# A new list of moves behind the front, four more key tiles for VectorE, and reads of two score banks at once

## The chip, the cores and the metric

The kernel runs on one core of one Trainium2 chip. The metric is the device time of one execution in microseconds; the median of three runs is 638.3 us (638.2 to 638.46).

## The reference

x is 2048 x 512. It is normalised row by row, goes through multi-query attention with 32 heads of 16 and one shared key and value head, and through a dense block of width 1792. The result is x + attention * silu(dense).

```python
xn = _layernorm(x, axis=-1)
q = (xn @ wq).reshape(B, S, H, Dh)                   # H = 32, Dh = 16
k, v = xn @ wk, xn @ wv
scores = jnp.einsum("bhqd,bkd->bhqk", q, k) * (Dh ** -0.5)
p = _softmax(scores, axis=-1)
s = jnp.einsum("bhqk,bkd->bhqd", p, v).transpose(0, 2, 1, 3).reshape(B, S, H * Dh) @ wo
h = _silu(jnp.einsum("bsd,df->bsf", xn, w1))
g = _silu(jnp.einsum("bsf,fd->bsd", h, w2))
return x + s * g
```

There are 2048 x 2048 x 32 scores, and each needs an exponential. That is most of the work.

## The kernel before

**Tiling.** The queries are cut into 4 chunks of 512 and the heads into 8 groups of 4, which makes 32 groups (chunk, heads). In each group the 2048 keys are cut into 16 key tiles of 128. A block is the scores of one key tile for one head: 128 keys by 512 queries, one PSUM bank of float32. One key tile of a group has 4 blocks, one for each head. The heads of 16 channels lie in strips of 32 rows, so TensorE is split into 4 row tiles for the scores (contraction over 32 rows, four heads side by side) and into 4 column tiles for everything that is summed over 128 rows.

**Two ways to the exponential.** The first is ScalarE. `fill_A` (L665) lets TensorE fill two blocks into psA, of which there are two copies of 1024 columns, and `exp_A` (L668, the activation is L674) takes the exponential of all 1024 columns into pa_sb. Two such steps make a key tile. The second is VectorE. `fill_block` (L1311) fills one block into one of four banks: D and D1 (the two halves of psD), F (psF) or O (psO). `exp_D` (L709, the instruction is L714) adds a constant to the scores, cuts at zero and writes 16-bit integers, which, read as bf16, are a rough exponential. When all four blocks of the tile are done, `shift` (L731, L739) makes POOL add a constant to the integers twice, which gives two copies that are shifted in phase; the three together, with weights in vaug_sb, approximate the exponential. So a key tile on ScalarE costs 2 exponentials and 4 matmuls against the values, and one on VectorE costs 4 reads on VectorE, 2 additions on POOL and 12 matmuls against the values.

**Quads.** `emit_quad` (L753, the matmul is L769) issues four such matmuls, one for each column tile, which run side by side into psO. `next_quad` (L1374) picks, for each of the four heads, the finished block with the earliest time `at` that the Python clock gave it. A dense quad (`emit_job`, L1049, through `columns`, L404) is likewise four matmuls side by side: the projection of q, the two layers of the dense block and the output projection. A change of TensorE between row tiles and column tiles happens at every alternation of a burst of score matmuls and a group of quads. The dense results go through tanh on ScalarE (L1116) and are multiplied on VectorE.

**Order.** Every engine works through its own queue in order. All queues are written out when the program is made, by `Sched.op`, which sets the semaphores from the data that an instruction reads and writes, and books a time for it on a clock in Python (`Sched.model`, L96). The clock itself leaves no instruction on the chip. Up to 30 us of booked ScalarE time a greedy planner picks the moves (the front); then `follow` (L1448) plays the moves written down in the string ORDER, and `finish` (L1378) those in TAIL. The letters that matter here:

- R0 or R1: fill psA for heads 0 and 1, or 2 and 3, of the next key tile; e: the exponential of it on ScalarE
- o: open a key tile for VectorE (taken from the end of the group's list), the second digit is one of four buffers; f: fill one block of it, the first digit is the bank (0 D, 1 D1, 2 F, 3 O), the second the tile and the head
- x: VectorE reads the oldest filled block; y: it reads the two oldest in one instruction of 1024 columns, which `exp_D` has a form for
- v: one quad against the values; J and d: open a dense job, and issue so many of its quads; t: its tanh; E: VectorE's step behind it
- 1 to 4: the four steps that normalise a group; H: one of the eight split bursts of the last group's first four key tiles, which `run_part` (L681, the matmul is L692) makes with parts of the queries; P, q, n and the rest: the last output rows

R and f that follow each other on TensorE's queue make one burst of row tiles, v and d one group of quads. A burst that comes to the same row tile twice needs a second pass.

Of the kernel before, what the change touches and what calls it, by code (L numbers as in the profile page):

```python
# [35 lines left out]
class Sched:  # L36
# [3 lines left out]
    SWITCH, FLY, SEM = 0.104, 0.172, 0.048  # L40

    def __init__(self):
        self.queues = {}
        self.done = {}
        self.clock = {}
        self.snap = {}
        self.last_w = {}
        self.readers = {}
        self.flagged = {}
        self.lanes = {}  # L50
        self.at = {}
        self.free = dict(pe=1.2, a=1.7, v=0.85, gp=0.7, sp=0.7)
        self.act_end = 0.0
        self.act_ends = []
        self.pe_mode, self.pe_last, self.pe_len, self.pe_tiles = None, 1.0, 0.0, set()
        self.pe_runs = []
        self.gp_runs, self.tt_runs = [], []

# [23 lines left out]
    def ready(self, eng, reads=(), writes=()):  # L82
        return max([self.at[d] for d in self.deps(eng, reads, writes).items()], default=0.0)
# [12 lines left out]
    def model(self, eng, lane, cost, r):  # L96
        if lane:
            t = max(self.free[eng], r) + 0.05
            self.free[eng] = t + (0.86 if eng == "gp" else 0.5)
            return t + (cost or 2.25)  # L100
        if eng == "pe":
            mode, tiles, cols = cost or ("full", [None] * 4, 128)
            t = r
            for tile in tiles:
                if mode != self.pe_mode:
                    t = max(t, self.pe_last + self.pe_len + self.SWITCH)
                    self.pe_tiles = set()
                elif tile is not None and tile not in self.pe_tiles:
                    t = max(t, self.pe_last + 0.004)
                else:  # L110
                    t = max(t, self.pe_last + self.pe_len + 0.003)
                    self.pe_tiles = set()
                self.pe_tiles.add(tile)
                self.pe_mode, self.pe_last, self.pe_len = mode, t, max(cols, 60) / 2400.0
                self.pe_runs.append((t, t + self.pe_len))
            self.free[eng] = t
            return t + cols / 2400.0 + self.FLY + self.SEM
        if eng == "a":
            n = cost or 512
            t = max(r, self.free["a"], self.act_end - 0.428)  # L120
            self.free["a"] = t
            self.act_end = max(t + 0.274 + n / 1200.0, self.act_end + 0.0635 + n / 1200.0)
            return self.act_end + self.SEM
        t = max(r, self.free[eng] - (0.084 if eng == "v" else 0.0))
        if eng == "v" and isinstance(cost, tuple):

            t = max(r, self.free[eng] - 0.13)
            end = t + cost[0]
            for a, b in self.gp_runs[-6:]:
                if a < t - 0.1:  # L130
                    end = max(end, b + cost[0] - 0.13)
            self.tt_runs.append((t, end))
            self.free[eng] = end
            return end + self.SEM
        end = t + (cost or 0.4)
        if eng == "gp" and cost and cost > 1.0:
            for a, b in self.tt_runs[-3:]:
                if a <= t + 0.1 and b > t:
                    end = max(end, b + 0.89)
            self.gp_runs.append((t, end))  # L140
        self.free[eng] = end
        return end + self.SEM

    def op(self, eng, fn, reads=(), writes=(), lane=None, cost=None):
        who = lane or eng
        if lane:
            self.lanes[lane] = eng
        n = self.done.get(who, 0)
        self.done[who] = n + 1
        deps = self.deps(eng, reads, writes)  # L150
        self.at[(who, n)] = self.model(eng, lane, cost, max([self.at[d] for d in deps.items()], default=0.0))
        clk = self.clock.setdefault(eng, {})
        waits = []
        cand = [(f, m) for f, m in deps.items() if clk.get(f, -1) < m]
        for f, m in cand:
            implied = False
            for f2, m2 in cand:
                if (f2, m2) != (f, m) and self.snap[(f2, m2)].get(f, -1) >= m:
                    implied = True
            if not implied:  # L160
                waits.append((f, m))
        for f, m in cand:
            for g, k in self.snap[(f, m)].items():
                if clk.get(g, -1) < k:
                    clk[g] = k
            if clk.get(f, -1) < m:
                clk[f] = m
        for f, m in waits:
            self.flagged.setdefault(f, set()).add(m)
        self.snap[(who, n)] = dict(clk)  # L170
        self.queues.setdefault(eng, []).append((fn, waits, who, n))
        for r in reads:
            self.readers.setdefault(r, {})[who] = n
        for w in writes:
            self.last_w[w] = (who, n)
            self.readers[w] = {}
        return who, n
# [36 lines left out]
def bass_recurrent_scan__grouped_kv_mqa__dense_activation_silu__prompt_kernel(  # L214
# [60 lines left out]
        K=(0.2, 3.0, 0.65, 10, 1.2, 2.0, 0, 24, 0.2, 3, 3, 0.0, 9, 0.43, 0, 0.33, 0, 0),  # L275
# [15 lines left out]
        a=(0.3, 3.0, 0.65, 10, 1.2, 2.0, -4, 24, 0.2, 3, 3, 0.04, 9, 0.43, 0, 0.33, 0, 0),  # L291
# [7 lines left out]
    TAIL = "vvHvvHPvvvvHHq0q0q0q0q1q1q1q1n0PPn1n0n1PPPq2q2q2n0n1n0q2PPr0r1n2C1n1n2n2G0Pr2Pn2PG2Pr3C3X1M1Y1A2A0M3Z1A3"  # L299
    ALPHA = "".join(chr(x) for x in range(35, 127) if x != 92) + "".join(chr(x) for x in range(192, 255))  # L300

    with ExitStack() as es:
        def sb(name, shape, dt=BF16):
# [44 lines left out]
        K = Sched()  # L348
        op = K.op


        op("gp", lambda e: e.memset(ident[:], 0.0), writes=["ident"])
        op("gp", lambda e: e.affine_select(out=ident[:], in_=ident[:], compare_op=ALU.not_equal, fill=1.0,
                                           base=0, pattern=[[-1, P]], channel_multiplier=1),
           reads=["ident"], writes=["ident"])
# [19 lines left out]
        for j in range(NPH + 1):  # L375
# [12 lines left out]
           reads=["wkn", "wkp"], writes=["wkp"])  # L388
# [7 lines left out]
        def load_w2():  # L396
            op("sp", lambda e: e.dma_start(of, xf), writes=["outx"], lane="lox", cost=20.0)
            op("sp", lambda e: e.dma_start(w2_sb[:], B_w2.rearrange("(ft p) n -> p ft n", p=P)), writes=["w2"], lane="lw2", cost=9.0)
# [229 lines left out]
        def bank_ap(b, m=NQ):  # L628
            if b == "O":
                return psO[:, :]  # L630
            return psF[:, :] if b == "F" else psD[:, NQ * (b == "D1"):NQ * (b == "D1") + m]
# [26 lines left out]
        def held(key):  # L658
            return waiting.get(key, 0) > 0
# [160 lines left out]
        def task(kind, run, cost, reads, writes, need=(), **kw):  # L820
            need = [n for n in need if not (n[0] in ("gn3", "gn4", "wmm", "add") and n[1] < 0)]
            tasks.append(dict(kind=kind, run=run, cost=cost, reads=reads, writes=writes, need=need, **kw))
# [289 lines left out]
        def emit_tanh():  # L1112
            jb, b = jst["tanh"].pop(0)
            n = state["nt"]
            state["nt"] += 1
            d = op("a", lambda e: e.activation(t_sb[:, n % 2, :], bank_ap(b), ACT.Tanh, scale=0.5 if jb[0] == "h" else 0.25),  # L1116
                   reads=[b], writes=[("t", n % 2)], cost=NQ)
            K.at[d] -= 0.06
            task(jb[0], evac, 0.679, jb=jb, bank=b, n=n, reads=[b, ("t", n % 2)], writes=[])
# [231 lines left out]
        def settled():  # L1351

            return not front and not shifts and all(("ag", t) in tok for t in tiles(NC - 1)) and ("kT", 1, NC - 1) in tok and K.act_end >= HANDOVER and \
                not any(tk["kind"] in ("st", "ag", "nm", "T", "K", "V") for tk in tasks)
# [154 lines left out]
        while not followed:  # L1509
# [3 lines left out]
            if not followed and settled():  # L1513
                if not w2_asked:
                    load_w2()
                    w2_asked = True
                follow(ORDER)
                followed = True
                continue
            t = max(now, min(K.pe_next("col"), K.pe_next("full")))  # L1520
# [7 lines left out]
            if tanh_ready(K.act_end - TGATE if more else t):  # L1528
                emit_tanh()
# [5 lines left out]
            if more:  # L1535
# [4 lines left out]
                if TWIN and K.pe_mode == "row" and not front and release() <= K.pe_next("row") + 0.12:  # L1540
                    slots, t = 0, K.pe_next("row")
# [5 lines left out]
            if slots > 0:  # L1547
                gi = state["g"]
                full = blocked or sum(held(("pa", k)) for k in range(NPA)) >= HOLD
# [7 lines left out]
                end = gi < NGRP and t >= gdone[gi] - PVWAIT and owed[gi] <= ENDQ  # L1557
# [23 lines left out]
            else:  # L1581
                now = 0.0
        finish(TAIL)
        last = {}
# [36 lines left out]
```

## Time and profile before

| | |
|---|---|
| median of 3 runs | 638.3 us |
| span of the profiled execution, first to last instruction | 635.8 us |
| TensorE matmuls busy | 628.8 us, 8227 |
| ScalarE busy | 625.9 us, 722 instructions |
| VectorE busy | 605.5 us, 1049 instructions |
| POOL busy | 435.6 us, 438 instructions |
| listed part, from its first burst to its last split burst | 29.5 to 622.7 us |

The page gives the span of the profiled execution and no other time of it. A row of the grouped view has line, engine, operation, output and inputs by name, shapes and count; then the busy time in us and the mean of one in ns; then the time for which the engine stood idle before them and what ended it. A row of the timeline has start and length in us, then the same names, and "x2" where rows that follow each other are drawn together. A sum over windows has for each engine the busy time in that stretch and the count.

### The profile page before, as it was taken

The numbers are of one execution on the slowest core, as the hardware profiler recorded it, in microseconds if no ns is written. First come the engines' busy times: TensorE is split into PE (matmuls) and PEld (weight loads), VectorE is DVE, ScalarE is ACT, GpSimd is POOL, SyncE is SP. The second block draws the span as 40 slices with busy tenths as digits, with TensorE's granted clock in tenths as the row PEclk, the third lists the DMA queues.
The fourth block names the chain that finished last, engine by engine and source line by source line (L and its number), as shares of the span: only waits on it lengthen the run. The fifth ranks groups of instructions, "written<-read, shape, count | busy, mean of one in ns | idle before, by whom it ended". The sixth has DMA issues, their size and how long they took to land.

```text
span 635.8 us, 18804 instructions
## 1 busy us (share of the span) xinstructions
PE 628.8 (99%) x8227; PEld 195.9 (31%) x8227; DVE 605.5 (95%) x1049; ACT 625.9 (98%) x722; POOL 435.6 (69%) x438
## 2 busy tenths in 40 slices
PE   8999999999999999999999999999999999999997
PEld 3433333332323222223223332223223233223323
DVE  8999999999999999999999999999999999999993
ACT  8999999999999999999999999999999999999996
POOL 6466665767667778777666876678767776776771
PEclk9999999999999999999999999999999999999999
DMA  6380000000000100000000000001000000000012
GB/s 185 117 283 2 2 2 2 2 3 1 2 2 2 19 1 11 10 2 2 1 3 2 1 3 2 2 10 18 10 3 2 2 2 1 3 1 2 3 18 53
DMA packets 10083, 12.51 MB, mean 20 GB/s; under 512 B 2288, under 2 KB 9456, under 8 KB 9968
## 3 DMA queue, kind: packets, MB, share of 16 engines
q1 hardware_dynamic: 7840, 9.34, 4.5%
q0 software_dynamic: 1728, 1.57, 2.1%
q8 instruction: 64, 1.05, 0.7%
q10 hardware_dynamic: 432, 0.39, 0.2%
q14 instruction: 19, 0.16, 0.1%
HBM read 8.95 MB, written 4.19 MB: 21 GB/s over the span
## 4 chain that ended last, share of the span: by engine, by line
PE 84%; ACT 9%; DVE 5%; DMA 0%; issue 0%
PE psO L769 32%; PE psA L643 27%; PE psF L404 20%; ACT pa_sb L674 8%; DVE ph_sb L714 3%; PE psD L643 2%; DVE x_sb L714 1%; ACT t_sb L1116 0%; PE psA L692 0%; DMA x_sb<-in_A_x_dram 0%; PE psD L507 0%; PE psD L476 0%; PE psF L643 0%; PE psD L533 0%; DVE stats_sb L424 0%
## 5 line engine op out<-in xcount | busy, mean ns | idle before, releaser
L674 ACT ACTIVATE pa_sb<-psA 128x1024 bf16<-128x1024 f32 x630 | 592.6, 1072 | 1.9 <-PE psA L643 0.6
L739 POOL INT64_ADD ph_sb<-ph_sb x304 | 316.5, 1056 | 131.2 <-DVE ph_sb L714 131.0
L714 DVE TENSOR_SCALAR ph_sb<-psD 128x512 int16<-128x512 f32 x521 | 336.5, 681 | 10.4 <-PE psD L643 8.5
L769 PE MATMUL psO<-ph_sb,vaug_sb 128*32 128x512 bf16 x1824 | 227.5, 383 | 0.1
L769 PE MATMUL psO<-pa_sb,vaug_sb 128*32 128x512 bf16 (+1 forms) x1292 | 201.5, 378 | 0.0
L643 PE MATMUL psA<-qT_sb,kTa_sb 32*128 32x512 bf16 x632 | 122.1, 384 | 0.1
L739 POOL INT64_ADD x_sb<-x_sb x90 | 93.3, 1055 | 41.6 <-DVE x_sb L714 41.4
L643 PE MATMUL psA<-qT_sb,kTb_sb 32*128 32x512 bf16 x612 | 118.4, 384 | 0.3 <-ACT pa_sb L674 0.3
L643 PE MATMUL psD<-qT_sb,kTb_sb 32*128 32x512 bf16 x335 | 113.5, 384 | 0.0
L643 PE MATMUL psD<-qT_sb,kTa_sb 32*128 32x512 bf16 x339 | 110.9, 385 | 0.0
L714 DVE TENSOR_SCALAR x_sb<-psD 128x512 int16<-128x512 f32 x153 | 100.8, 682 | 6.1 <-PE psD L643 5.3
L769 PE MATMUL psO<-x_sb,vaug_sb 128*32 128x512 bf16 x540 | 96.4, 383 | 0.0
L769 PEld LDWEIGHTS psO<-ph_sb,vaug_sb 128*32 128x32 bf16 x1824 | 55.8, 95 | 57.5 <-issue 35.1
L643 PEld LDWEIGHTS psA<-qT_sb,kTa_sb 32*128 32x128 bf16 x632 | 29.7, 91 | 122.0 <-ACT pa_sb L674 92.2
L404 PE MATMUL psF<-w_sb,u_sb 128*32 128x512 bf16 x896 | 66.2, 384 | 0.0
L643 PEld LDWEIGHTS psA<-qT_sb,kTb_sb 32*128 32x128 bf16 x612 | 28.7, 91 | 121.0 <-ACT pa_sb L674 98.1
L404 PE MATMUL psF<-xnT_sb,w_sb 128*32 128x512 bf16 x896 | 64.7, 383 | 0.0
L769 PEld LDWEIGHTS psO<-pa_sb,vaug_sb 128*32 128x32 bf16 x1292 | 50.2, 95 | 33.5 <-issue 24.2
L714 DVE TENSOR_SCALAR ph_sb<-psF 128x512 int16<-128x512 f32 x70 | 47.7, 681 | 0.0
L1116 ACT ACTIVATE t_sb<-psF 128x512 bf16<-128x512 f32 x72 | 45.9, 638 | 0.0
L1135 DVE SCALAR_TENSOR_TENSOR u_sb<-t_sb,psF 128x512 bf16<-128x512 bf16 x56 | 38.0, 678 | 0.2
L643 PEld LDWEIGHTS psD<-qT_sb,kTa_sb 32*128 32x128 bf16 x339 | 28.8, 91 | 2.3 <-DVE ph_sb L714 0.4
(121 smaller groups left out, 397.1 us busy)
## 6 DMA issues: line engine op xcount, KB each, us to landing
w_sb<-in_B_w_dram SPq DMA_DIRECT2D x2, 1792.0 KB, 10.9
x_sb<-in_A_x_dram SPq DMA_DIRECT2D x3, 512.0 KB, 5.2
out_dram<-ob_sb POOLq DMA_DIRECT2D x12, 128.0 KB, 3.0
wop_sb<-in_A_wo_dram SPq DMA_DIRECT2D x1, 512.0 KB, 4.1
wq_sb<-in_A_wq_dram SPq DMA_DIRECT2D x1, 384.0 KB, 6.1
out_dram<-ob_sb SPq DMA_DIRECT2D x3, 128.0 KB, 2.4
x_sb<-in_A_x_dram SPq DMA_DIRECT2D x2, 128.0 KB, 2.6
x_sb<-in_A_x_dram ACTq DMA_DIRECT2D x2, 128.0 KB, 2.8
```

What stands on the lines that cost most here:

```text
L404: r = e.matmul(bank[32 * i:32 * i + 32, :], lhsT=w, rhs=rhs, start=start, stop=stop, tile_position=(0, 32 * i), skip_group_check=True)
L643: return e.matmul(ap, lhsT=kT_sb[g % 2][32 * i:32 * i + 32, kt * P:(kt + 1) * P], rhs=qT_sb[32 * i:32 * i + 32, c % 2, g // 2, :], start=T ...
L674: d = op("a", lambda e: e.activation(pa_sb[:, sl, :], psA[k][:, :], ACT.Exp, scale=ESCALE), reads=["A%d" % k], writes=[("pa", sl)], cost=2 ...
L714: d = op("v", lambda e: e.tensor_scalar(ph_ap(0, sl, 512 * pos, 512 * pos + m), src, float(PH_ONE + PH_BIAS), 0.0, op0=ALU.add, op1=ALU.ma ...
L739: d = op("gp", lambda e, j=j: e.int64_add(ph_ap(j, sl, 0, 4 * NQ).bitcast(I64), ph_ap(0, sl, 0, 4 * NQ).bitcast(I64), PH_SHIFT[j] * 0x0001 ...
L769: r = e.matmul(psO[32 * i:32 * i + 32, cs], lhsT=vaug_sb[:, p["v"], p["kt"], DH * (gi % 2):DH * (gi % 2) + 32], rhs=p["ap"], start=s0, sto ...
L1116: d = op("a", lambda e: e.activation(t_sb[:, n % 2, :], bank_ap(b), ACT.Tanh, scale=0.5 if jb[0] == "h" else 0.25), reads=[b], writes=[("t ...
L1135: op("v", lambda e: e.scalar_tensor_tensor(out=dst, in0=t_sb[:, n % 2, :], scalar=1.0, in1=src, op0=ALU.add, op1=ALU.mult), reads=tk["read ...
```

## The change

The class of the clock gets a second mode, `fine`, which is switched on just before `follow`. In it a dependency between TensorE and VectorE, and between VectorE and POOL, has a lag of its own; TensorE, ScalarE, VectorE and POOL are booked with other constants; and the result of a tanh is put earlier by 0.022 instead of 0.06. ORDER is replaced as a whole, and TAIL has three more quads between the sixth and the seventh split burst. The functions that play the moves are unchanged.

Counted from the two strings:

| moves in ORDER | before | after |
|---|---|---|
| e, exponentials of 1024 columns (H included) | 605 | 597 |
| R, fills of psA | 601 | 593 |
| o, key tiles for VectorE | 195 | 199 |
| f, fills for VectorE: D, D1, F, O | 783: 335, 335, 90, 23 | 799: 329, 329, 108, 33 |
| x, reads of one block | 784 | 704 |
| y, reads of two blocks | 0 | 48 |
| v, quads against the values | 887 | 892 |
| dense quads | 556 | 556 |
| t, tanh | 72 | 72 |
| groups of quads between bursts | 595 | 569 |
| of 1, 2, 3, 4, 5, 6 quads | 76, 263, 183, 73, 0, 0 | 122, 164, 182, 58, 38, 5 |
| bursts with two fills of psA | 10 | 28 |
| second passes in bursts | 11 | 31 |
| quads in TAIL against the values, before its last split bursts | 8 | 11 |

Of the 48 places with y, the next burst fills F alone among VectorE's banks in 43, O alone in 3, D and D1 in one and none in one.

```diff
@@ -38,6 +38,7 @@
 
 
     SWITCH, FLY, SEM = 0.104, 0.172, 0.048
+    LAG = {("pe", "v"): 0.0325, ("v", "gp"): 0.0405}
 
     def __init__(self):
         self.queues = {}
@@ -55,6 +56,10 @@
         self.pe_mode, self.pe_last, self.pe_len, self.pe_tiles = None, 1.0, 0.0, set()
         self.pe_runs = []
         self.gp_runs, self.tt_runs = [], []
+        self.fine, self.pe_pos = False, 0
+
+    def when(self, d, eng):
+        return self.at[d] + (self.LAG.get((d[0], eng), 0.0) if self.fine else 0.0)
 
     def deps(self, eng, reads, writes):
         deps = {}
@@ -80,7 +85,7 @@
         return deps
 
     def ready(self, eng, reads=(), writes=()):
-        return max([self.at[d] for d in self.deps(eng, reads, writes).items()], default=0.0)
+        return max([self.when(d, eng) for d in self.deps(eng, reads, writes).items()], default=0.0)
 
     def activity(self, t, window=3.4):
 
@@ -98,6 +103,24 @@
             t = max(self.free[eng], r) + 0.05
             self.free[eng] = t + (0.86 if eng == "gp" else 0.5)
             return t + (cost or 2.25)
+        if eng == "pe" and self.fine:
+            mode, tiles, cols = cost or ("full", [None] * 4, 128)
+            t = r
+            for tile in tiles:
+                end = self.pe_last + self.pe_len
+                if mode != self.pe_mode:
+                    t = max(t, end + (0.098 if mode == "row" else 0.1012))
+                    self.pe_tiles, self.pe_pos = set(), 0
+                elif tile is not None and tile not in self.pe_tiles:
+                    t = max(t, self.pe_last + 0.0033)
+                else:
+                    self.pe_pos += 1
+                    t = max(t, end + (0.003 if mode != "col" or self.pe_pos == 1 else -0.0075))
+                    self.pe_tiles = set()
+                self.pe_tiles.add(tile)
+                self.pe_mode, self.pe_last, self.pe_len = mode, t, max(cols, 60) / 2400.0
+            self.free[eng] = t
+            return t + cols / 2400.0 + 0.2125
         if eng == "pe":
             mode, tiles, cols = cost or ("full", [None] * 4, 128)
             t = r
@@ -115,6 +138,12 @@
                 self.pe_runs.append((t, t + self.pe_len))
             self.free[eng] = t
             return t + cols / 2400.0 + self.FLY + self.SEM
+        if eng == "a" and self.fine:
+            n = cost or 512
+            t = max(r, self.free["a"], self.act_end - 0.428)
+            self.free["a"] = t
+            self.act_end = max(t + 0.1707 + n / 1200.0, self.act_end + 0.0632 + n / 1200.0)
+            return self.act_end + 0.055
         if eng == "a":
             n = cost or 512
             t = max(r, self.free["a"], self.act_end - 0.428)
@@ -131,15 +160,15 @@
                     end = max(end, b + cost[0] - 0.13)
             self.tt_runs.append((t, end))
             self.free[eng] = end
-            return end + self.SEM
+            return end + (0.0565 if self.fine else self.SEM)
         end = t + (cost or 0.4)
         if eng == "gp" and cost and cost > 1.0:
             for a, b in self.tt_runs[-3:]:
                 if a <= t + 0.1 and b > t:
                     end = max(end, b + 0.89)
             self.gp_runs.append((t, end))
-        self.free[eng] = end
-        return end + self.SEM
+        self.free[eng] = end - (0.02 if self.fine and eng == "gp" else 0.0)
+        return end + (0.0565 if self.fine else self.SEM)
 
     def op(self, eng, fn, reads=(), writes=(), lane=None, cost=None):
         who = lane or eng
@@ -148,7 +177,7 @@
         n = self.done.get(who, 0)
         self.done[who] = n + 1
         deps = self.deps(eng, reads, writes)
-        self.at[(who, n)] = self.model(eng, lane, cost, max([self.at[d] for d in deps.items()], default=0.0))
+        self.at[(who, n)] = self.model(eng, lane, cost, max([self.when(d, eng) for d in deps.items()], default=0.0))
         clk = self.clock.setdefault(eng, {})
         waits = []
         cand = [(f, m) for f, m in deps.items() if clk.get(f, -1) < m]
@@ -295,8 +324,8 @@
     NF, F_FROM, F_LEFT, F_LATE, DENSE_END, HOLD, F_BEHIND = 14, 0.05, 9, 3, 0.97, 10, 0
 
     HANDOVER = 30.0
-    ORDER = "xvR0eJ#2d1R1f11f00ed3xxR0o02f16evE#vR1f01exJ$2d2xR0f13ed2xvE$R1f00f11eR0xeJ%2d4xR0o13f02f13eE%vxR1eJ&2d4xR1f00f11tev
...
-R1f01f20evxR0f13evxvvxR1f01eJÄ2d2xR0o00f12ed2xR1f00eEÄvvxR0f13eJÅ2d1xvR1f01ed3xR0o01f12eEÅvR1f00exJÆ2d31R0f13exvvxR1f01ed1xvR0o02f12e2vEÆvR1f00exJÇ2d2xR0f13ed13vxR1f01ed1xvvHeEÇvvHevvHevvHe"
-    TAIL = "vvHvvHPvvvvHHq0q0q0q0q1q1q1q1n0PPn1n0n1PPPq2q2q2n0n1n0q2PPr0r1n2C1n1n2n2G0Pr2Pn2PG2Pr3C3X1M1Y1A2A0M3Z1A3"
+    ORDER = "R0xf11f01exJ$2d2R1xf10exd2R0E$o02f03evvR1xf10evR0xf22o03f07evxvf11xR1eJ#2d2xR0f02exd2vR1E#f10f01evxvR0xo02f12evR1xf2
...
+f03evxvvR0xf12o03f23xevvvR1xf00evR0xf12evxvR11f01eJÃ2d3R1x2o00f10f31ed1d1R0xxf02ed3R0xf13ed1R1xo01f01f30exd2f12xR0exd3vvR13o02f04f15teR1xevvvxvvEÃvR0f03f12evHexJÇ2xd3vd1HeEÇvf03HeJÆ2xd4HeEÆ"
+    TAIL = "vvHvvHPvvvvvvvHHq0q0q0q0q1q1q1q1n0PPn1n0n1PPPq2q2q2n0n1n0q2PPr0r1n2C1n1n2n2G0Pr2Pn2PG2Pr3C3X1M1Y1A2A0M3Z1A3"
     ALPHA = "".join(chr(x) for x in range(35, 127) if x != 92) + "".join(chr(x) for x in range(192, 255))
 
     with ExitStack() as es:
@@ -1115,7 +1144,7 @@
             state["nt"] += 1
             d = op("a", lambda e: e.activation(t_sb[:, n % 2, :], bank_ap(b), ACT.Tanh, scale=0.5 if jb[0] == "h" else 0.25),
                    reads=[b], writes=[("t", n % 2)], cost=NQ)
-            K.at[d] -= 0.06
+            K.at[d] -= 0.022 if K.fine else 0.06
             task(jb[0], evac, 0.679, jb=jb, bank=b, n=n, reads=[b, ("t", n % 2)], writes=[])
 
         def add_x(tt, src, key):
@@ -1514,6 +1543,7 @@
                 if not w2_asked:
                     load_w2()
                     w2_asked = True
+                K.fine = True
                 follow(ORDER)
                 followed = True
                 continue
```

2 lines of the change are left out of this document (1 added, 1 removed).

## The prediction

> **What bounds the kernel now.** I read the page first: the shares of the engines, the chain that ended last and the costliest groups.
>
> ```profile
> span 635.8 us, 18804 instructions
> PE 628.8 (99%) x8227; PEld 195.9 (31%) x8227; DVE 605.5 (95%) x1049; ACT 625.9 (98%) x722; POOL 435.6 (69%) x438
> ...
> PE 84%; ACT 9%; DVE 5%; DMA 0%; issue 0%
> ...
> L674 ACT ACTIVATE pa_sb<-psA 128x1024 bf16<-128x1024 f32 x630 | 592.6, 1072 | 1.9 <-PE psA L643 0.6
> L739 POOL INT64_ADD ph_sb<-ph_sb x304 | 316.5, 1056 | 131.2 <-DVE ph_sb L714 131.0
> L714 DVE TENSOR_SCALAR ph_sb<-psD 128x512 int16<-128x512 f32 x521 | 336.5, 681 | 10.4 <-PE psD L643 8.5
> ...
> L714 DVE TENSOR_SCALAR x_sb<-psD 128x512 int16<-128x512 f32 x153 | 100.8, 682 | 6.1 <-PE psD L643 5.3
> ```
>
> Three engines are over 95%. Then the sums over windows: all of the listed part (29.4 to 620), and the stretch where VectorE is fullest.
>
> ```profile
> core 0: us, PE busy (x) PEld busy (x) DVE busy (x) ACT busy (x) POOL busy (x), PEclk, DMA share, GB/s
> 29.40:620.00 590.60, 590.14 (x7733) 177.79 (x7729) 573.52 (x960) 589.42 (x674) 415.93 (x404) 1.00 0.05 12
> ...
> 200.00:300.00 100.00, 99.54 (x1295) 29.51 (x1291) 99.16 (x168) 100.00 (x114) 75.67 (x74) 1.00 0.05 7
> ```
>
> In the listed part ScalarE stands still for 1.2 us of 590.6 and VectorE for 17.1 us; TensorE's clock is full. ScalarE's instructions overlap, so its floor has to come from the pitch, which a timeline shows:
>
> ```profile
> 299.48 0.60 ACT L1116 ACTIVATE t_sb<-psF 128x512 bf16<-128x512 f32 x1
> ...
> 299.95 3.79 ACT L674 ACTIVATE pa_sb<-psA 128x1024 bf16<-128x1024 f32 x4
> ...
> 613.29 12.98 ACT L674 ACTIVATE pa_sb<-psA 128x1024 bf16<-128x1024 f32 x14
> ```
>
> Fourteen exponentials in 12.98 us, the last 1.07 long: a pitch of (12.98 - 1.07)/13 = 0.916 us. A tanh holds the engine for 299.95 - 299.48 = 0.47, say 0.48 us. The old list has 605 exponentials and 72 tanh: 605 x 0.916 + 72 x 0.48 = 588.8 us.
>
> TensorE needs its own count, since its busy share hides waits. The timeline of TensorE alone shows its rhythm, a burst of score matmuls (psA, psD) and then quads:
>
> ```profile
> 602.69 0.39 PE L643 MATMUL psA<-qT_sb,kTa_sb 32*128 32x512 bf16 x2
> ...
> 603.56 0.39 PE L643 MATMUL psA<-qT_sb,kTa_sb 32*128 32x512 bf16 x2
> ...
> 605.30 0.39 PE L643 MATMUL psA<-qT_sb,kTa_sb 32*128 32x512 bf16 x2
> ...
> 606.45 0.39 PE L643 MATMUL psA<-qT_sb,kTa_sb 32*128 32x512 bf16 x2
> 606.56 0.38 PE L643 MATMUL psD<-qT_sb,kTb_sb 32*128 32x512 bf16 x1
> ...
> 607.21 0.39 PE L643 MATMUL psA<-qT_sb,kTb_sb 32*128 32x512 bf16 x2
> ...
> 608.30 0.39 PE L643 MATMUL psA<-qT_sb,kTb_sb 32*128 32x512 bf16 x2
> ```
>
> A burst with two quads takes 0.87 (602.69 to 603.56, and 605.30 - 602.69 is three of them), with three quads 1.09 (607.21 to 608.30). So a further quad is 0.22, and a burst with one quad 0.65; a second pass in a burst, one more set of 512 columns, I put at 0.21. At 606.56 the psD fill begins 0.11 after its burst where others follow at once: it waits inside the burst for VectorE to give the bank back, and this counts as busy. The old list has 595 groups of quads with 1443 quads and 11 second passes: 595 x 0.648 + 848 x 0.22 + 11 x 0.21 = 574.5 us. Its first and last burst:
>
> ```profile
> 29.49 0.39 PE L643 MATMUL psA<-qT_sb,kTa_sb 32*128 32x512 bf16 x2
> ...
> 620.09 0.39 PE L692 MATMUL psA<-qT_sb,kTb_sb 32*128 32x256 bf16 x4
> ...
> 622.69 0.39 PE L692 MATMUL psA<-qT_sb,kTb_sb 32*128 32x256 bf16 x4
> ...
> 626.02 0.70 PE L692 MATMUL psA<-qT_sb,kTb_sb 32*128 32x128 bf16 x16
> ```
>
> 622.69 - 29.49 = 593.2 us. ScalarE's floor is 4.4 us below that, TensorE's 18.7 us. So ScalarE sets the pace, and what TensorE has left over goes into waits inside its bursts.
>
> **The change, part by part.** *Four more key tiles to VectorE.* ScalarE loses 8 exponentials: 8 x 0.916 = 7.3 us, all of it on the path that sets the pace. VectorE gets 16 blocks, POOL 8 additions (8.4 us at 1056 ns on an engine that is 69% busy and so hides them; without cover each would make its quad late by a microsecond), TensorE 8 quads net of the list and the tail (1.8 us).
>
> *The new grouping on TensorE.* 569 groups, 1448 quads, 31 second passes: 569 x 0.648 + 879 x 0.22 + 31 x 0.21 = 368.7 + 193.4 + 6.5 = 568.6 us, 5.9 less than before. 26 fewer alternations give it; the second passes take back 4.2. Against ScalarE's new floor, 597 x 0.916 + 72 x 0.48 = 581.4, TensorE then has 12.8 us for waits instead of 14.3: ScalarE stays the pace setter as long as waits do not grow.
>
> *Blocks read two at a time.* No instruction of the trace reads two blocks, so its price is bounded:
>
> ```profile
> 251.02 1.89 DVE L714 TENSOR_SCALAR ph_sb<-psD 128x512 int16<-128x512 f32 x3
> ...
> L484 DVE COPY xnT_sb<-psD 128x1024 bf16<-128x1024 bf16 x4 | 2.7, 682 | 0.0
> ...
> L519 DVE CAST kTa_sb<-psD 128x256 bf16<-128x256 f32 x4 | 1.7, 413 | 0.0
> ...
> L519 DVE CAST kTa_sb<-psO 128x384 bf16<-128x384 f32 x1 | 0.6, 558 | 0.0
> ```
>
> Singles follow each other at (1.89 - 0.68)/2 = 0.60. From 256 to 384 columns a read of the same source type grows by 145 ns, to 512 (681) by 268: 1.05 ns a column. 512 more columns are 0.54, so a pair holds VectorE for 0.60 + 0.54 = 1.14 and saves 0.06 against two singles. Low end: 1024 columns of 16 bits in 682 ns, no dearer than one single. High end: two singles with no overlap, 1.36. I take 1.14, since source type and form are nearest. VectorE's change is 16 x 0.60 - 48 x 0.06 = +6.7 us; low end 9.6 - 28.8 = -19.2, high end 9.6 + 48 x 0.16 = +17.3. At +6.7 it is 580.2 us busy in some 585: cover that is thin. [...]
>
> *The new clock.* It runs while the program is made. On the chip it changes only which finished blocks a quad takes, since the list fixes the rest. A wait that it gets rid of could be worth up to ScalarE's 4.4 us; a wrong choice makes a quad wait for a copy, up to the 1.06 us that one addition takes on POOL, in front of all later bursts, since TensorE's queue is in order, and ScalarE waits for those. Between a gain of 4.4 and a loss of some such waits I take nothing: the old list stands only 4.4 above its floor, so wrong choices were rare in it.
>
> *The end.* The last D block is now filled between the second and third split burst, so its shifted copies come late and their quads stand behind. From first to seventh split burst the old order has groups of 2, 2, 2, 2, 2 and 5 quads: 6 x 0.648 + 9 x 0.22 = 5.9 us (trace: 626.02 - 620.09 = 5.93). The new one has 5, 1, 4, 2, 2 and 8: 3.9 + 16 x 0.22 = 7.4 us. ScalarE wants 6 x 0.916 = 5.5 for them, so it starves there by 1.5 us more. Some can be absorbed if TensorE arrives ahead, by at most one exponential less the 0.45 from fill to use; I take +1.3.
>
> Sum: -7.3 + 1.3 = -6.0 by ScalarE; by TensorE with equal waits -5.9 + 3 x 0.22 = -5.2. I take -5.8: the profiled span 635.8 becomes 630.0. The page gives no other time of that execution; the median of the runs, 638.3, lies 2.5 above the span, and I keep that: 632.5 us.
>
> **The rivals.** *The waits go too.* With the lags right, ScalarE's 4.4 us of residue falls to about 1 and TensorE's waits follow: 632.5 - 3.5 = 629.0. For it: waits in bursts are often short, as the 0.11 at 606.56. Against: VectorE is fuller than before, and residue this small is hard to cut.
>
> *VectorE becomes the bound.* If it can be no denser than in the window from 200 to 300 (99.16%), its 580.2 us take 585.1 instead of 590.6; with the end's 1.3 that is -4.2, 634.1 us. For it: the added 6.7 us take more than a third of the 17.1 us that VectorE has idle in the whole listed part. Against it: in that window ScalarE is 100% busy all the same, so a VectorE with 0.84 us idle in 100 did not slow it. [...]
>
> *Slower: a pair holds both banks of psD.* A single gives its bank back after 0.68 us; a pair keeps both to its end. If nothing else is filled by then, VectorE stands until a refill:
>
> ```profile
> 30.16 0.39 PE L643 MATMUL psD<-qT_sb,kTb_sb 32*128 32x512 bf16 x2
> ...
> 30.62 1.29 DVE L714 TENSOR_SCALAR ph_sb<-psD 128x512 int16<-128x512 f32 x2 [0.96 <-PE psD L643]
> ```
>
> From fill to read 0.46 us, and some 0.06 from release to fill: 0.52 a pair. With half of the 48 pairs uncovered, 24 x 0.52 = 12.5: 645 us. It decides from 11 uncovered pairs on (5.8/0.52). Against it: in the new list 43 of the 48 pairs are followed by a burst that fills psF and 3 by one that fills psO. The high end of the pair's price, 1.36, works out alike: 573.5 + 17.3 = 590.8 busy, at 99.16% 595.8, plus 1.3 at the end: 645 too.
>
> *No gain.* TensorE's waits grow by what the exponentials give, 5.9 us, because fuller VectorE returns banks later: 638.3.
>
> **How the numbers follow.** Chances: forecast 0.50 (own range 630.5 to 634), waits go too 0.16, VectorE the bound 0.13, slower by banks or a dear pair 0.14, no gain 0.07. A measurement of this kernel can tell about 0.2%, 1.3 us, from no change. Faster 0.79, same 0.07, slower 0.14. Range 628.5 to 638.8: it holds the forecast, the two faster rivals and no gain; left out are most of the slow case and a few hundredths below, since ScalarE without any residue is 638.3 - 7.3 - 4.4 + 1.3 = 627.9.
>
> **What would show it.** The exponentials: 622 on line 674, pitch 0.916. VectorE: 48 reads of 1024 columns, near 1.22 us each; waits for psD fills not above the present 8.5 and 5.3 us. TensorE: fills of psD inside bursts waiting no more in sum, the run from first to seventh split burst about 7.4 us, 0.5 to 1 us idle on ScalarE before the seventh. I am wrong if ScalarE, in the listed part, shows several microseconds idle before psA, if a pair takes 1.3 us or more, or if the gaps of VectorE after pairs add up to over 5 us.

## The result and the profile after

| | before | after |
|---|---|---|
| median | 638.25 us (637.72 to 638.46) | 630.87 us (630.52 to 631.36) |
| span of the profiled execution | 635.8 us | 629.4 us |

The ratio is 0.9888, 95% interval 0.9874 to 0.9902: 7.1 us faster by the ratio, 7.4 by the medians. The prediction was 632.5 us, that is 5.8 faster. In the new code the lines stand 29 further down: L674 is L703, L714 is L743, L739 is L768, L643 is L672, L692 is L721.

The page of the new kernel, the lines that answer to those of before:

```profile
span 629.4 us, 18825 instructions
...
PE 621.7 (99%) x8257; PEld 199.6 (32%) x8259; DVE 612.0 (97%) x1017; ACT 618.9 (98%) x714; POOL 443.5 (70%) x446
...
PE 72%; ACT 24%; DVE 2%; DMA 1%; issue 0%; SPq 0%
...
L703 ACT ACTIVATE pa_sb<-psA 128x1024 bf16<-128x1024 f32 x622 | 583.5, 1058 | 2.5 <-PE psA L721 1.3
...
L743 DVE TENSOR_SCALAR ph_sb<-psD 128x512 int16<-128x512 f32 (+1 forms) x462 | 320.6, 723 | 4.4 <-PE psD L672 3.5
...
L743 DVE TENSOR_SCALAR x_sb<-psD 128x512 int16<-128x512 f32 (+1 forms) x152 | 106.0, 717 | 0.9 <-PE psD L672 0.6
```

The eight exponentials are gone (630 to 622). VectorE's share went from 95% to 97%, although it has more work: its waits for a filled psD fell from 8.5 + 5.3 us to 3.5 + 0.6. The chain of work that ended last still lies on TensorE for most of the span, 72% after 84% before. The sum over the listed part, from its first burst at 29.88 to its first split burst at 612.90:

```profile
core 0: us, PE busy (x) PEld busy (x) DVE busy (x) ACT busy (x) POOL busy (x), PEclk, DMA share, GB/s
29.90:612.90 583.00, 582.11 (x7741) 180.88 (x7738) 577.75 (x925) 582.23 (x666) 420.65 (x408) 1.00 0.05 12
```

VectorE stood still for 17.1 us of 590.6 before; now it is 5.3 of 583.0 (583.00 - 577.75). ScalarE has 0.8 idle. The timeline of TensorE gives the ends of the stretches:

```profile
29.88 0.39 PE L672 MATMUL psA<-qT_sb,kTa_sb 32*128 32x512 bf16 x2
...
612.90 0.39 PE L721 MATMUL psA<-qT_sb,kTb_sb 32*128 32x256 bf16 x4
...
620.28 0.31 PE L721 MATMUL psA<-qT_sb,kTb_sb 32*128 32x128 bf16 x8
```

Between first burst and first split burst lie 583.0 us, against 590.6 (620.09 - 29.49) before: -7.6. From the first to the seventh split burst it is 7.38 us (620.28 - 612.90) against 5.93: +1.45. The front, whose code is the same, ended 0.4 later in this execution, and what follows the seventh split burst was 0.7 shorter (9.1 against 9.8). The four make -6.4, the difference of the spans.

### The profile page after: what moved, and what is told of

The parts are those of the page before. It is cut to its first block, busy times and chain, and to the rows that moved or that the text cites. A ratio compares the mean times of both kernels' runs of the same rounds, so it can differ in the third digit from the quotient of the medians.

```text
span 629.4 us, 18825 instructions
## 1 busy us (share of the span) xinstructions
PE 621.7 (99%) x8257; PEld 199.6 (32%) x8259; DVE 612.0 (97%) x1017; ACT 618.9 (98%) x714; POOL 443.5 (70%) x446
## 3 DMA queue, kind: packets, MB, share of 16 engines
q8 instruction: 64, 1.05, 0.7%
## 4 chain that ended last, share of the span: by engine, by line
PE 72%; ACT 24%; DVE 2%; DMA 1%; issue 0%; SPq 0%
PE psO L798 28%; PE psA L672 22%; ACT pa_sb L703 22%; PE psF L433 17%; PE psD L672 2%; ACT t_sb L1145 2%; DMA x_sb<-in_A_x_dram 1%; DVE ph_sb L743 0%; PE psF L672 0%; PE psD L536 0%; PE psD L505 0%; PE psA L721 0%; PE psD L562 0%; ACT xnT_sb L526 0%; DVE onb_sb L901 0%
## 5 line engine op out<-in xcount | busy, mean ns | idle before, releaser
L703 ACT ACTIVATE pa_sb<-psA 128x1024 bf16<-128x1024 f32 x622 | 583.5, 1058 | 2.5 <-PE psA L721 1.3
L768 POOL INT64_ADD ph_sb<-ph_sb x302 | 314.0, 1060 | 118.7 <-DVE ph_sb L743 118.3
L743 DVE TENSOR_SCALAR ph_sb<-psD 128x512 int16<-128x512 f32 (+1 forms) x462 | 320.6, 723 | 4.4 <-PE psD L672 3.5
L798 PE MATMUL psO<-pa_sb,vaug_sb 128*32 128x512 bf16 (+2 forms) x1276 | 205.5, 379 | 0.2 <-ACT pa_sb L703 0.2
L768 POOL INT64_ADD x_sb<-x_sb x100 | 104.1, 1057 | 41.6 <-DVE x_sb L743 41.4
L672 PE MATMUL psA<-qT_sb,kTb_sb 32*128 32x512 bf16 x616 | 118.8, 384 | 0.2 <-ACT pa_sb L703 0.2
L672 PE MATMUL psA<-qT_sb,kTa_sb 32*128 32x512 bf16 x612 | 116.5, 384 | 0.2
L672 PE MATMUL psD<-qT_sb,kTa_sb 32*128 32x512 bf16 x350 | 107.1, 384 | 0.5 <-DVE x_sb L743 0.5
L743 DVE TENSOR_SCALAR x_sb<-psD 128x512 int16<-128x512 f32 (+1 forms) x152 | 106.0, 717 | 0.9 <-PE psD L672 0.6
L798 PE MATMUL psO<-x_sb,vaug_sb 128*32 128x512 bf16 x600 | 105.1, 383 | 0.0
L672 PE MATMUL psD<-qT_sb,kTb_sb 32*128 32x512 bf16 x312 | 95.3, 384 | 0.0
L672 PEld LDWEIGHTS psA<-qT_sb,kTb_sb 32*128 32x128 bf16 x616 | 28.9, 91 | 109.3 <-ACT pa_sb L703 93.2
L672 PEld LDWEIGHTS psA<-qT_sb,kTa_sb 32*128 32x128 bf16 x612 | 28.7, 91 | 104.7 <-ACT pa_sb L703 78.5
L743 DVE TENSOR_SCALAR ph_sb<-psF 128x512 int16<-128x512 f32 x80 | 54.5, 681 | 0.1
L798 PEld LDWEIGHTS psO<-x_sb,vaug_sb 128*32 128x32 bf16 x600 | 26.6, 95 | 20.1 <-issue 11.5
```

Source lines behind the costliest of these rows:

```text
L672: return e.matmul(ap, lhsT=kT_sb[g % 2][32 * i:32 * i + 32, kt * P:(kt + 1) * P], rhs=qT_sb[32 * i:32 * i + 32, c % 2, g // 2, :], start=T ...
L703: d = op("a", lambda e: e.activation(pa_sb[:, sl, :], psA[k][:, :], ACT.Exp, scale=ESCALE), reads=["A%d" % k], writes=[("pa", sl)], cost=2 ...
L743: d = op("v", lambda e: e.tensor_scalar(ph_ap(0, sl, 512 * pos, 512 * pos + m), src, float(PH_ONE + PH_BIAS), 0.0, op0=ALU.add, op1=ALU.ma ...
L768: d = op("gp", lambda e, j=j: e.int64_add(ph_ap(j, sl, 0, 4 * NQ).bitcast(I64), ph_ap(0, sl, 0, 4 * NQ).bitcast(I64), PH_SHIFT[j] * 0x0001 ...
L798: r = e.matmul(psO[32 * i:32 * i + 32, cs], lhsT=vaug_sb[:, p["v"], p["kt"], DH * (gi % 2):DH * (gi % 2) + 32], rhs=p["ap"], start=s0, sto ...
```

## Experiments

The prediction had a theory of the pace, called the ScalarE theory here: ScalarE is full, TensorE and VectorE have something left over, so the time follows the exponentials. Its rivals are the clock theory (the right clock made the gain), the TensorE theory (the saved alternations made it) and, from the second half of the runs on, the tied theory: three engines in step, each of which holds up the next. Ratios are to the kernel before; microseconds are worked out from them with 638.3. A difference of two such ratios is known to about 1 us.

### Is it the clock?

`e1_clock_only` takes the new file and puts the old strings back; `e2_list_only` leaves the switch out.

```diff
-    ORDER = "R0xf11f01exJ$2d2R1xf10exd2
...
+    ORDER = "xvR0eJ#2d1R1f11f00ed3xx
...
```

```diff
-                K.fine = True
```

> The old ORDER and TAIL, played with the new clock: only the choice of the blocks that a quad takes can differ from the kernel before. ScalarE theory (the 8 exponentials made the gain, the clock by itself nothing): 637.6 to 639.0 us. Clock theory (right times let quads take blocks that are ready, and waits go): 634 to 636.5 us.

Measured: 637.84 us, ratio 1.0007 (0.9996 to 1.0017).

> The new ORDER and TAIL, played with the old clock. ScalarE theory: 630.2 to 632.0 us, as after. Clock theory: 633 us or more, since the choices of blocks are wrong again.

Measured: 630.72 us, ratio 0.9892 (0.9876 to 0.9907), as after. The clock does change the choice of blocks: with the old list, 274 of TensorE's 8227 matmuls read another tile than those at the same place before. But these choices are worth less than the measurement can tell. The whole difference that can be measured is in the two strings.

### The reads of two banks

```diff
...
-R1xo01f04f15yevR0f23evvvR0xf02f13evyvR1
+R1xo01f04f15xxevR0f23evvvR0xf02f13evxxvR1
...
```

> Each of the 48 reads of two banks becomes two reads of one. VectorE gets 48 x 0.06 = 2.9 us more. ScalarE theory (VectorE still has some 11 us idle in the listed part): 630.5 to 632.0 us. VectorE-bound rival: 633.8 us or more. Rival that pairs hold both banks too long: under 630 us.

Measured: 633.02 us, ratio 0.9927 (0.9915 to 0.9939), so 2.5 us slower than after. That lies between what the ScalarE theory and the rival with VectorE as the bound expected. The expectation spoke of some 11 us idle on VectorE; the sum above has 5.3. The forms kept apart, in the profile after:

```profile
L743 DVE TENSOR_SCALAR ph_sb<-psD 128x512 int16<-128x512 f32 x425 | 275.5, 680 | 4.3 <-PE psD L672 3.5 <-PE psA L721 0.3
...
L743 DVE TENSOR_SCALAR ph_sb<-psD 128x1024 int16<-128x1024 f32 x37 | 45.1, 1220 | 0.1
...
L743 DVE TENSOR_SCALAR x_sb<-psD 128x1024 int16<-128x1024 f32 x11 | 13.4, 1217 | 0.0
```

A pair takes 1.22 us, and the next instruction starts some 0.08 before its end, so it holds VectorE for 1.14, as estimated. It saves 0.06 against two singles, 48 x 0.06 = 2.9 us, and about 2.5 of it is lost with the pairs. The listed part without pairs, 585.2 us long:

```profile
30.20:615.40 585.20, 584.34 (x7740) 183.06 (x7736) 579.99 (x973) 584.03 (x666) 421.16 (x408) 1.00 0.05 12
```

VectorE's idle time stayed the same, 5.2 us (585.20 - 579.99), although 5.3 would have held 2.9 more. What grew is TensorE's waits inside bursts, from 11.5 to 14.1 us in sum. (Such a wait is counted here where a score matmul of the listed part starts 0.02 to 0.2 us behind the one before it in its burst.) So VectorE's time counted almost in full, though the sums showed it idle.

### What a microsecond more costs on each engine

Three kernels add work to after, spread over the listed part, and leave all other queues as they are: 16 small exponentials on ScalarE, 33 quads of zeros on TensorE, 12 row statistics on VectorE. What they add changes no result. The edits, in this order, and the added rows from the profiles:

```diff
+            if K.fine and n % 37 == 20:
+                was = K.free["a"], K.act_end
+                op("a", lambda e: e.activation(wkp_sb[:, :, :].rearrange("p c e -> p (c e)"), zero_sb[:, :], ACT.Exp, scale=ESCALE),
+                   reads=["zero"], writes=["wkp"], cost=NQ)
+                K.free["a"], K.act_end = was
...
+                    if more and m == end:
+                        columns(e, ap, zero_sb[:, 0:P], zero_sb[:, :], False, False)
...
+            if K.fine and n % 50 == 30:
+                was = K.free["v"]
+                op("v", lambda e: e.bn_stats(stats_sb[:, 0, :], zero_sb[:, :]), reads=["zero"], writes=[("st", 0)], cost=0.687)
+                K.free["v"] = was
```

```profile
L708 ACT ACTIVATE wkp_sb<-zero_sb 128x512 bf16<-128x512 bf16 x16 | 10.9, 684 | 0.0
```

```profile
L433 PE MATMUL psF<-zero_sb 128*32 128x512 bf16 x132 | 12.9, 380 | 0.0
```

```profile
L708 DVE BATCH_NORM_STATS2 stats_sb<-zero_sb 128x6 f32<-128x512 bf16 x12 | 8.2, 680 | 0.0
```

> After, with 16 exponentials of 512 columns more on ScalarE, of an SBUF row of zeros into a tile that nothing reads any more, spread over the listed part; the other queues are as in after. About 16 x 0.49 = 7.8 us of ScalarE. ScalarE theory: +6.5 to +8 us, 637.4 to 638.9. TensorE theory (the 26 alternations saved made the gain): at most +3, under 634.

Measured: 638.31 us, ratio 1.0001 (0.9992 to 1.0011): +7.2 us for 7.8.

> After, with one quad of zeros more in every third dense job, 33 in all, 33 x 0.22 = 7.3 us of TensorE; the result of the job does not change. ScalarE theory (TensorE has some 18 us of waits that can shrink): +1 to +3 us, 632 to 634. TensorE theory: +6 to +7.3, 637 to 638.2.

Measured: 637.31 us, ratio 0.9984 (0.9975 to 0.9994): +6.1 us for 7.3.

> After, with 12 row statistics of zeros more on VectorE, 512 columns each, pitch 0.60: 7.2 us, into a tile that nothing reads any more. ScalarE theory (VectorE has about 11 us idle, but little of it where it is wanted): +1 to +4 us, 632 to 635. VectorE-bound rival: +6 to +7.2, 637 to 638.

Measured: 636.98 us, ratio 0.9973 (0.9963 to 0.9984): +5.4 us for 7.2.

ScalarE and TensorE did what the theory that makes each of them the bound expected, and VectorE came close to it: 5.4 us lies between the 1 to 4 of the ScalarE theory and the 6 to 7.2 of its rival. Not all three can be the only bound. The listed part with TensorE's, and then with VectorE's extra work:

```profile
29.40:619.00 589.60, 588.43 (x7872) 183.75 (x7868) 580.29 (x925) 585.88 (x666) 420.63 (x408) 1.00 0.05 12
```

```profile
29.40:618.60 589.20, 585.86 (x7739) 181.49 (x7736) 584.17 (x937) 584.45 (x666) 420.45 (x408) 1.00 0.05 12
```

ScalarE's idle time rises from 0.8 to 3.7 (589.60 - 585.88) and to 4.8 us (589.20 - 584.45); the ends of its exponentials, which show lost overlap too, lie 6.6 and 6.3 us further apart in sum. ScalarE, busy for 582.23 of 583.00 us in after, did not make this up. And an engine's own idle time did not take up the work that was added to it: VectorE's 5.3 us are still 5.0 (589.20 - 584.17), and TensorE's waits inside bursts, 155 of 11.5 us in sum after, are 153 of 11.9 with the extra quads. They are no reserve here. The likely reason, which no run takes apart, is that VectorE's read comes after TensorE's fill, so that when the fill is late the release of the bank moves along.

### What a microsecond less brings

If adding to any engine costs, taking away from one might bring nothing. `e7_before_act_minus16` and `e10_after_act_minus16` halve 16 exponentials (6.8 us of ScalarE; in the profile of e7 they last 0.65 us instead of 1.07), `e8_before_pe_minus32` leaves out 32 dense quads (7.1 us of TensorE), `e9_before_dve_minus15` cuts 15 reads from 512 to 64 columns (7 us of VectorE; in the profile of e9 0.22 us each instead of 0.68). The parts of the result that hang on them are left out.

```diff
-            d = op("a", lambda e: e.activation(pa_sb[:, sl, :], psA[k][:, :], ACT.Exp, scale=ESCALE),
+            m = NQ if n > 37 and n % 37 == 20 else 2 * NQ
+            d = op("a", lambda e: e.activation(pa_sb[:, sl, 0:m], psA[k][:, 0:m], ACT.Exp, scale=ESCALE),
...
+            less = 1 if jb in listed[::3] and 1 in items and len(items) > 1 else None
...
+                    if m == less:
+                        continue
...
+            u = 64 if idx > 12 and idx % 13 == 0 and pos == 2 else m
```

> The kernel before, with 16 of its exponentials on only the first 512 of 1024 columns; the second half of those 16 tiles is left out. ScalarE is relieved of 16 x 0.427 = 6.8 us, nothing else changes. ScalarE theory: 5 to 7 us faster than before. Tied theory (three engines in step, each extra microsecond costs on any of them, so relief of one alone is lost at the next): 0 to 2.5 us faster.

Measured: 638.51 us, ratio 1.0000 (0.9991 to 1.0009).

> The kernel before, with one quad left out in 32 dense jobs, 32 x 0.22 = 7.1 us of TensorE relieved; those products are left out of the result. ScalarE theory: at most 1 us faster. TensorE theory: 6 to 7 us faster. Tied theory: 0 to 2.5 us faster.

Measured: 638.12 us, ratio 0.9996 (0.9988 to 1.0005).

> The kernel before, with 15 of VectorE's reads on only 64 of 512 columns, 15 x 0.47 = 7 us of VectorE relieved; the other columns of those blocks are left out. ScalarE theory: at most 1 us faster. Tied theory: 0 to 2.5 us faster.

Measured: 638.37 us, ratio 0.9998 (0.9989 to 1.0007).

> After, with the same 16 half exponentials, 6.8 us of ScalarE relieved, the second half of those tiles left out. ScalarE theory: 5 to 7 us faster than after, 624 to 626. Tied theory: 0 to 2 us, 629 to 631, since VectorE has only some 11 us idle left there.

Measured: 630.69 us, ratio 0.9880 (0.9867 to 0.9894), as after.

Some 7 us less on any one engine of the old list, or on ScalarE in the new one, bring nothing that can be measured (the intervals of e7 to e9 are 0.6 us wide on each side). The ScalarE theory falls with e7, the TensorE theory with e8. The sum over the listed part of e7 shows where the 6.8 us are: ScalarE 584.99 busy and 5.6 idle, where before had 1.2.

```profile
29.40:620.00 590.60, 589.97 (x7722) 177.81 (x7714) 573.47 (x958) 584.99 (x673) 414.69 (x404) 1.00 0.05 12
```

One of the 16 places in the timeline of that run; the last of the three exponentials in the first row is a shortened one and ends at 250.34:

```profile
247.86 2.48 ACT L675 ACTIVATE pa_sb<-psA 128x1024 bf16<-128x1024 f32 x3
...
248.83 1.87 DVE L715 TENSOR_SCALAR ph_sb<-psD 128x512 int16<-128x512 f32 x3
...
249.23 0.39 PE L643 MATMUL psA<-qT_sb,kTa_sb 32*128 32x512 bf16 x2
249.56 0.09 PEld L643 LDWEIGHTS psD<-qT_sb,kTa_sb 32*128 32x128 bf16 x1 [0.24 <-DVE ph_sb L715]
...
250.21 0.39 PE L643 MATMUL psA<-qT_sb,kTa_sb 32*128 32x512 bf16 x2
...
250.64 1.02 ACT L675 ACTIVATE pa_sb<-psA 128x1024 bf16<-128x1024 f32 x1 [0.30 <-PE psD L643]
```

ScalarE is done 0.30 early and stands. Its next input was filled at 250.21. TensorE could not fill it earlier, for the burst before, begun at 249.23, had waited until 249.56 for VectorE to release a bank. Before, ScalarE works through the same place without a gap:

```profile
247.67 6.63 ACT L674 ACTIVATE pa_sb<-psA 128x1024 bf16<-128x1024 f32 x7
```

So here VectorE held TensorE, and TensorE held ScalarE, in a place where ScalarE was just busy enough before to hide it. The other 15 places were not followed one by one.

### Two and three engines at once

The last two relieve the engines of the old list at the same places. Where a dense quad is left out (7.1 us of TensorE), the next exponential is halved (12.8 us of ScalarE), and in the second kernel VectorE's next read is cut to 64 columns too (13.6 us). What hangs on these is again left out of the result.

```diff
+            m = NQ if state["half"] else 2 * NQ
+            state["half"] = False
...
+            u = 64 if state["short"] and idx > 8 else m
+            state["short"] = False
...
+            if less and state["n"] > 37:
+                state["half"] = state["short"] = True
```

> The kernel before, relieved on two engines at the same places: one quad left out in 32 dense jobs (7.1 us of TensorE), and the next exponential behind 30 of them on half of its columns (12.8 us of ScalarE); both are left out of the result. Tied theory with ScalarE and TensorE as the two chains: 3 to 7 us faster than before, at most TensorE's 7.1. If VectorE is a third chain of the same length: under 2 us faster.

Measured: 635.99 us, ratio 0.9971 (0.9959 to 0.9982): 1.9 us faster.

> As the run with two engines, and VectorE's next read at 29 of these places on 64 of 512 columns (13.6 us of VectorE), left out too. If VectorE is a third chain: 4 to 7 us faster than before, and 2 or more faster than with two engines relieved. If it is not: as with two. If one fixed loop of waits sets the time, whatever the engines' work: under 1 us in both.

Measured: 632.85 us, ratio 0.9922 (0.9909 to 0.9936): 5.0 us faster.

One engine relieved: nothing. Two: 1.9 (1.1 to 2.6) of the 7.1 us that TensorE, the least relieved, was spared. Three: 5.0 (4.1 to 5.8). This is what the tied theory with VectorE as the third chain expected, with two close to its limit of 2 us. In the run with two, ScalarE took much of its relief as idle time (7.9 us, 589.90 - 582.00):

```profile
29.40:619.30 589.90, 589.15 (x7617) 176.54 (x7616) 574.58 (x962) 582.00 (x675) 416.65 (x404) 1.00 0.05 12
```

VectorE with only one of the others was not relieved, and VectorE alone only by half as much and at other places (e9). So the runs show that relief of VectorE adds 3.1 us to that of the other two, and not that all three have to be relieved.

## Why the prediction came out right, and where it was wrong

**The terms of the sum.** The exponentials were put at -7.3 us, and the listed part up to the split bursts got 7.6 shorter. The end was put at 7.4 us from first to seventh split burst, 5.9 before, and at +1.3 net; it measured 7.38 and +1.45. ScalarE's idle before the seventh, put at 0.5 to 1 us, stands in its timeline as 1.06 (second row):

```profile
614.85 4.81 ACT L703 ACTIVATE pa_sb<-psA 128x1024 bf16<-128x1024 f32 x5 [0.23 <-PE psA L721]
620.72 1.94 ACT L703 ACTIVATE pa_sb<-psA 128x1024 bf16<-128x1024 f32 x2 [1.06 <-PE psA L721]
```

The two stretches make -6.1, where -6.0 by ScalarE and -5.2 by TensorE with equal waits had been worked out and -5.8 taken. TensorE's waits inside bursts did not stay equal: 198 of 16.3 us before, 155 of 11.5 after. Another 0.7 us no step of the prediction had: the last copy on ScalarE begins 5.8 us after the seventh split burst in both profiles, but the span ends 9.8 after it before and 9.1 now, as the last store lands 1.7 us after its issue instead of 2.5.

Three of the smaller terms can be read from the traces. A second pass was an estimate of 0.21 us; in after the shortest bursts with one last 0.53 to 0.55 us up to the next quad, and those without 0.32 in the median. The way from release to fill, put at 0.06, is 0.06 in the trace of before, and the one from fill to use, put at 0.45, is 0.43 there where ScalarE had waited.

One term was mis-sized. The 2.5 us for what lies outside the span came from a median and from the span of another execution, a faster one. In every execution whose time and span are both on record, the difference is 1.7 to 1.9 us; the profiled one after has 631.2 - 629.4 = 1.8. By an estimate from this, the execution on the page before took some 637.6 us. So the span, forecast at 630.0, missed by 0.6, and the time, forecast at 632.5, by 1.6.

**The step that failed.** "So ScalarE sets the pace, and what TensorE has left over goes into waits inside its bursts." ScalarE is always fed, but it does not set the pace alone: 6.8 us less on it brought nothing (e7). And what TensorE seemed to have left over, 18.7 us before and 12.8 by the count for the new list, was not free: 7.3 us more on TensorE cost 6.1 (e5). ScalarE, TensorE and VectorE are chains that hold each other up. The prediction showed a sign of it, the chain that ended last with 84% on TensorE and 9% on ScalarE, and did not answer it.

The size came out because both lists keep ScalarE fed: with 1.2 and 0.8 us idle, the listed part can only be as long as ScalarE's work and what little overlap is lost. What it takes to keep ScalarE fed, the prediction left out of its sum. TensorE loses 5.9 us by the count of groups, and its waits inside bursts fall by 4.8, of which some 3 come back as waits elsewhere. VectorE gets four tiles more, and yet its idle time falls by 11.8 us (17.1 to 5.3). That the new list gave the other two engines about what it took from ScalarE was not forecast, and in that respect the agreement is luck. The same sum would have forecast e7 5 to 7 us faster, and been wrong by all of it. None of the signs of being wrong that the prediction named came: ScalarE shows 1.2 and 0.8 us of idle time in the two lists, although it does not set the pace alone.

**VectorE's cover.** The 6.7 us were costed as hidden, with a thin cover, and 580.2 us busy. It measured 577.75, in part because two reads now come behind the first split burst. They are hidden in the list that was made for them. Work that was put in without fitting, on the same engine in the same list, cost 5.4 of 7.2 us (e6), and the list without pairs 2.5 of 2.9 (e3). The pairs were costed right in size (1.14 us) and wrong in effect: in this list they are a third of the gain.

**The clock** was costed at nothing, and e1 and e2 show nothing. **The rivals:** the slower one, that a pair holds both banks of psD, did not come: VectorE stands for 0.0 us in sum behind the 48 pairs, and without pairs the kernel is slower. VectorE as the bound was right in that VectorE's time counts: over the listed part it is now 99.1% busy (577.75 of 583.00), as dense as that rival thought possible. With the busy time that was measured, its own rule gives 582.6 us for the listed part (577.75/0.9916), and 583.0 were measured; its 634.1 came from the 580.2. But that VectorE alone would count is not what the runs show: more work on ScalarE or on TensorE costs as well, and with TensorE's extra work VectorE stands still for 9.3 us (589.60 - 580.29). The rival that waits go too was right about TensorE's waits inside bursts and wrong about the cause, the clock, and about ScalarE: what the listed part has above ScalarE's floor by the count was 5.5 us before (590.6 - 601 x 0.916 - 72 x 0.48) and is 5.2 now (583.0 - 593 x 0.916 - 72 x 0.48).

**What stays open.** Within the new list, how much belongs to the eight exponentials and how much to the 26 alternations saved was not taken apart: no list was run that has one without the other. In the new list only ScalarE was relieved, so whether less work on VectorE or TensorE alone would make it faster is not known.

## What to carry to other kernels

When several engines are nearly full, as the three were before at 95, 98 and 99%, add a little to each and take a little from each before you call one of them the bound. Here adding to any of the three cost some three quarters of the added time or more, and taking from one brought nothing. On these runs relief of ScalarE alone, 98% busy, was worth nothing, of ScalarE and TensorE at the same places 0.3%, and of all three 0.8%.

An order that is fixed when the program is made does not adapt. In this one, work put in without a new plan cost most of its time, and work taken out of one engine brought nothing. So plan such a change with the queues of all engines laid out anew.

## What the runs showed of the hardware that was not expected

Waits of TensorE for a bank inside a burst were no slack: with 7.3 us more to do (e5), they stayed at 11.5 to 11.9 us in sum, and the time rose by 6.1.

A read of 1024 columns across the two banks of psD cost what its columns cost, with no extra price for the second bank: 1.22 us against 0.68 for 512, so 512 columns more took 0.54, the same 1.05 ns a column by which reads of 256 and 512 columns differ in the profile before (413 and 681 ns).
